# A fused attention and expert kernel on one core: the next attention's loads traced two units sooner, its first copies in program order, small columns made later

## The chip, the cores and the metric

The kernel runs on one core of a Trainium2 chip. The metric is device time in microseconds (us) of one execution. Before the change three runs gave 713.15, 713.35 and 713.98, a median of 713.35. One further execution was recorded by the hardware profiler, and all rows below come from it.

## The reference

Causal attention with a cumulative bias, then two feed-forward layers: a dense one, and four experts whose outputs are added by normalised shares.

```python
# attention: q, k, v (2, 8, 576, 64), s (2, 8, 576)
scores = (q @ k.T) / sqrt(64)
cum    = cumsum(max(s, 0));  bias = -(cum[:, None] - cum[None, :])
scores = where(causal, -1e9, scores + minimum(bias, 0))
attn   = exp(scores - max);  attn /= attn.sum(-1) + 1e-9
x      = (attn @ v)                       # (1152, 512) after joining the heads
# layer 1: w_in (512, 2048), w_out (2048, 512)
h = x @ w_in;  x = where(h > 0, h, exp(min(h, 0)) - 1) @ w_out
# layer 2: 4 experts, w1 (4, 512, 1024), w2 (4, 1024, 512), shares (1152, 4)
p = domain_probs / (domain_probs.sum(-1) + 1e-9)
out = sum over e of p[:, e] * (max(x @ w1[e], 0) @ w2[e])
```

## The kernel before

The 1152 tokens are worked in three groups of 256, 448 and 448. `attention_first` makes the attention of the first group alone. After it `layer1` runs over 16 units of the first layer's weights (a unit is a slice of 128 of the 2048 hidden columns), and then a loop over 32 units (16 to 47) of the expert weights makes layer 2 of the first group. While these 48 units run for the first group, the attention of the second group is made in the background, a few steps per unit. The rest of the program repeats this for the other two groups and is not touched.

**Units.** `slot` traces one unit: the up product (`up1` in layer 1, `up2` in layer 2), then `advance`, which fetches and prepares weights for later units, then the down product of the unit two before (`LAG`). In layer 1 of the first group the weights arrive coded: `fetch_halves` loads 32 halves of 512 KB, `decode_halves` turns each into floats with two ACT and two DVE instructions (L150, L157, L158, L160), and every finished unit is written to HBM (`w_dec`) from POOL's queue for the later groups. Layer 2's units come as plain floats: `fetch` (L97, tile `raw`, 512 KB) is called for unit n + 4 in `advance(n)`, and `prepare` (L103, L87) splits them into a high half on ACT and a low half on DVE (tile `wu`), which the up product needs.

**The background attention.** `attention_parts` returns a list of steps, and `Background` calls them at an even pace between the first and the last unit that `BG_FROM` and `BG_TO` set. The first step, `start`, issues the loads of the eight small pieces (tile `pt`: q, k and v of 128 tokens) and of the first two jobs (tiles `q`, `k`, `cbp`, `v`), 21 DMAs that are all placed behind the last coded half on SP's queue. It also calls `split` for the first item: three copies on ACT (`qs` L478, `kh` L479, `qb` L481) and two subtractions on DVE, which make high and low parts of q and k.

**Order.** The program is traced in the order of the Python code, and a scheduler then may reorder each engine's instructions, with its own picture of how long things take. `tc.keep_in_program_order` forbids this for one instruction; `tc.issue_after` puts a block's instructions behind a given one on its engine. Each engine then works strictly through its list, so an instruction that waits holds up everything after it. SP's list is the DMA queue of all loads; one DMA is issued only when the eighth before it has landed, so there are at most eight under way.

**Small columns.** `cum_columns` makes, with one TensorE transpose and four DVE copies each, columns of the cumulative sums that later items with 64 tokens need. `probabilities_of` loads the experts' shares and normalises them in four small DVE instructions. Before the change both stand in the middle of the first attention.

Of the kernel before, what the change touches and what calls it, by code (L numbers as in the profile page):

```python
# [12 lines left out]
AF = mybir.ActivationFunctionType  # L13
# [21 lines left out]
T2 = GROUPS[1][0]  # L35
NCH = 2 * N2 // 128
# [3 lines left out]

LAG = 2

BG_FROM = [14, 0, 0]
BG_TO = [1, 1, 0]

DEC = [1, 2, 3, 4]
# [7 lines left out]
def tile_kernel(ctx, tc, qT, kT, v, s, w64, w, probs, out):  # L54
# [13 lines left out]
    PE, DVE, ACT, POOL, SP = nc.tensor, nc.vector, nc.scalar, nc.gpsimd, nc.sync  # L68
# [6 lines left out]
    def sb(shape, tag, bufs, dtype=F32):  # L75
        p = (base if tag in BASE else edge if tag in EDGE else l1_pool if tag in L1
             else att_pool[0])
        return p.tile(shape, dtype, tag=tag, name=tag, bufs=bufs)
# [4 lines left out]
    def ps_att():  # L83
        return ps("att", 2)
# [24 lines left out]
    small = [("yh", 1, 1), ("yl", 1, 1)] + [("raw", 3, 1)] * 3 + [("xa", 1, 3), ("ox", 1, 3)]  # L109
# [105 lines left out]
    def cum_columns(b, i):  # L215

        c0, c1 = CHUNKS[b][i], CHUNKS[b][i + 1]
        src, t = sb([B * H, 2, 64], "cum_2", 2), cum_t[b]
        for j in range(2):
            DVE.tensor_copy(src[:, j], cum[:, c0:c1])  # L220
        pt = ps_att()
        PE.transpose(pt[:, :B * H], src.rearrange("p a b -> p (a b)"), ident[:B * H, :B * H])
        DVE.tensor_copy(t, pt[:, :B * H])
        for j in range(2):
            r = slice(64 * j, 64 * j + 64)
            heads = t[r, b * H:(b + 1) * H].rearrange("p (a j) -> p j a", j=2)
            DVE.tensor_copy(cum_p[b][r], heads[:, j])
# [15 lines left out]
    def probabilities_of(t0, n):  # L243

        pr = sb([128, NCH, E], "pr", 2)[:, :n]
        POOL.dma_start(out=pr, in_=probs[t0:t0 + 128 * n].rearrange("(t p) e -> p t e", p=128))
        prs = sb([128, NCH, 1], "prs", 1)[:, :n]
        DVE.tensor_reduce(prs, pr, AX.X, ALU.add)
        DVE.tensor_scalar(prs, prs, 1e-9, None, op0=ALU.add)
        DVE.reciprocal(prs, prs)  # L250
        DVE.tensor_tensor(out=pr, in0=pr, in1=prs.to_broadcast([128, n, E]), op=ALU.mult)
        return pr


    shares = []

    def attention_first(x):


        n = 256  # L260
# [19 lines left out]
        parts, less = (sb([80, n], t, 1, F32R) for t in ("cump", "cumm"))  # L280
# [3 lines left out]
        for t, sign in ((parts, 1.0), (less, -1.0)):  # L284
            POOL.tensor_copy(t[:64], zero)
            high = ACT.activation(t[:B * H], cum[:, 0:n], AF.Copy, scale=sign)
            low = DVE.scalar_tensor_tensor(out=t[64:], in0=cum[:, 0:n], scalar=sign,
                                     in1=t[:B * H].bitcast(F32), op0=ALU.mult, op1=ALU.subtract)
# [9 lines left out]
        def scores(hp):  # L298
            for j in range(2):
                h = 2 * hp + j  # L300
                banks[h] = ps(f"acc{h % 4}", 1) if h < 4 or h > 5 else ps("up", 2)
            for d0, d1 in chunks:
                for j in range(2):
                    r = slice(64 * j, 64 * j + 64)
                    PE.matmul(banks[2 * hp + j][:, d0:d0 + d1], qkv[r, 0, hp, d0:d1],
                              qkv[r, 1, hp, 0:d1], start=d0 == 0, stop=False,
                              skip_group_check=True)
            for j in range(2):
                h = 2 * hp + j
                one = ones[:, h:h + 1]  # L310
                for d0, d1 in chunks:
                    o = banks[h][:, d0:d0 + d1]
                    PE.matmul(o, one.to_broadcast([80, 128]), parts[:, 0:d1],
                              start=False, stop=False, skip_group_check=True)
                    last = PE.matmul(o, less[:, d0:d1], one.to_broadcast([80, d1]),
                                     start=False, stop=d0 > 0, skip_group_check=True)
            return last
# [11 lines left out]
        def normalise(hp):  # L329
            r = sm[:, :, 2 * hp:2 * hp + 2]  # L330
            DVE.tensor_scalar(r, r, 1e-9, None, op0=ALU.add)
            DVE.reciprocal(r, r)
            for h in (2 * hp, 2 * hp + 1):
                for i, (d0, d1) in enumerate(chunks):
                    p = pp[h][:, d0:d0 + d1]
                    scaled = DVE.tensor_scalar(p, p, sm[:, i, h:h + 1], None, op0=ALU.mult)
            return scaled
# [25 lines left out]
            return last  # L363

        with tc.issue_after(keep_warm(12).ins):
            first = scores(0)
            with tc.issue_after(first.ins), tc.issue_after(low.ins):
                cum_columns(0, 4)
                cum_columns(1, 4)
            scores(1)  # L370
            scores(2)
        probabilities(0)
        decode_halves(DEC[0])
        with tc.issue_after(scores(3).ins):
            keep_warm(6)
        probabilities(1)
        with tc.issue_after(normalise(0).ins):
            shares.extend((probabilities_of(0, n // 128), probabilities_of(T2, NCH)))
        with tc.issue_after(transposes(0).ins):
            keep_warm(4)  # L380
        probabilities(2)
# [6 lines left out]
        transposes(2)  # L388
        values(1)
        decode_halves(DEC[2])  # L390
        normalise(3)
        transposes(3)
        values(2)
        values(3)
# [3 lines left out]
    def attention_parts(g, x):  # L398


        items, jobs, small = [], [], []
        for b, chunks, col in JOBS[g]:
            cb = CHUNKS[b]
            q0, q1 = cb[chunks[0]], cb[chunks[-1] + 1]
            for hp in range(HP):
                job = dict(b=b, chunks=chunks, col=col, q0=q0, q1=q1, hp=hp)
# [57 lines left out]
        def split(it):  # L464


            job, j = it["job"], it["j"]
            if j is None or (j, "q") in job:
                return
            q, k = job["q"][:, j], job["k"][:, j]  # L470
            qs = sb([128, q.shape[-1]], "qs", 2, F32R)
            kh = sb([128, k.shape[-1]], "kh", 2, F32R)
            qb = sb([68, q.shape[-1]], "qb", 2, F32R)
            kl = sb([68, k.shape[-1]], "kl", 2, F32R)
            h = job["b"] * H + 2 * job["hp"] + j
            SP.dma_start(out=qb[64:].bitcast(F32), in_=rows_d[h, 2:6, job["q0"]:job["q1"]])
            SP.dma_start(out=kl[64:].bitcast(F32), in_=rows_d[h, 0:4, 0:job["q1"]])
            ACT.activation(qs, q, AF.Copy)  # L478
            ACT.activation(kh, k, AF.Copy)  # L479
            split_lo(qs[64:], q[64:], qs[64:])  # L480
            ACT.activation(qb[:64], q[:64], AF.Copy)  # L481
            split_lo(kl[:64], k[:64], kh[:64])
            job[j, "q"], job[j, "qb"], job[j, "kh"], job[j, "kl"] = qs, qb, kh, kl

# [17 lines left out]
        def normalise():  # L502
            while norm:
                p, sm = norm.pop(0)
                DVE.tensor_scalar(sm, sm, 1e-9, None, op0=ALU.add)
                DVE.reciprocal(sm, sm)
                DVE.tensor_scalar(p, p, sm, None, op0=ALU.mult)

        def scores(it, cut):
            job, i, j = it["job"], it["i"], it["j"]  # L510
            b, hp = job["b"], job["hp"]
            cb = CHUNKS[b]
            d0, d1 = cb[i], cb[i + 1]
            a, e, first, last = cut
            normalise()
            pss = ps_att()
            qk(it, pss, a, e)
            if first:
                it["p"] = sb([128, d1], "p", 4)
                it["low"] = 3.0e38  # L520
                if j is None:
                    it["bias"] = sb([128, d1], "bias", 2)
                    add_bias(it["bias"], job["cump"][:, 0], cum_p[b][:, hp:hp + 1], d0, d1, maskp)
                else:
                    it["bias"] = mask[:, S - d1:]
            p, nm = it["p"], sb([128, 1], "nm", 8)
            DVE.tensor_tensor_reduce(p[:, a:e], pss[:, :e - a], it["bias"][:, a:e], -1.0 / SC,  # L527
                                     it["low"], ALU.add, ALU.min, nm)
            it["low"] = nm
            if last:  # L530
                sm = sb([128, 1], "sm", 4)
                ACT.activation(p, p, AF.Exp, bias=nm, scale=-1.0, accum_out=sm)  # L532
                norm.append((p, sm))
# [46 lines left out]
        def start():  # L580
            with late():
                if small:
                    load_small()
                for job in jobs[:2]:
                    load(job)
            split(items[0])

        parts = [start, lambda: None]
        for n in range(len(items) + 2):
            if n < len(items):  # L590
                it = items[n]
# [158 lines left out]
    class First:  # L750
# [3 lines left out]
        def __call__(self, at):  # L754
            if at > BG_FROM[0]:
                if self.got is None:
# [3 lines left out]
                    xs[1] = sb([128, 2, NCC, N2], "xa", 1, F32R)  # L760
                    self.got = Background(attention_parts(1, xs[1]), BG_FROM[0],
                                          NAB + LAG + E * NCD - BG_TO[0])
# [328 lines left out]
```

## Time and profile before

| What | Value |
|---|---|
| profiled execution, time | 712.33 us |
| its span, first to last instruction | 710.5 us |
| median of three runs | 713.35 us |
| TensorE (PE) busy | 695.7 us, 98% |
| weight loads of TensorE (PEld) busy | 594.1 us, 84% |
| VectorE (DVE) busy | 561.8 us, 79% |
| ScalarE (ACT) busy | 366.9 us, 52% |
| mean granted TensorE clock | 0.997 |
| moved by DMA over the span | 97 MB, mean 137 GB/s |

The shares are means over stages with different limits: in the first 95 us DMA moves three times its mean and ACT and DVE are nearly full, while from 400 us on ACT is a third busy. All that the change touches lies in the first 140 us, so the rows to read are those of that stretch: the timeline of each engine, the list of waits, and windows of a few microseconds. A busy matmul in the record also covers pipelining, so starts of successive blocks tell the pace better than their durations.

### The profile page before, as it was taken

To read this page: it belongs to the slowest core of one execution; us is meant where nothing else is said; L and a number is where in the kernel's file an instruction comes from. 1 tells how busy PE (TensorE), PEld (TensorE's weight loads), DVE (VectorE), ACT (ScalarE), POOL (GpSimd) and SP (SyncE) were. 2 spreads that over 40 slices of the span, in tenths; PEclk is the share of its full clock that TensorE was granted. 3 is DMA by queue.
4 is the path that set the end of the run, shared out by engine and by line. 5 is a ranking of instruction groups with operands and counts; after the bars stand their busy time and mean duration, and the time that the engine had idled before them with its cause. 6 is when DMAs were issued, how large, how long until landed. Compare 5 with 4: busy or idle time off the path is not lost.

```text
span 710.5 us, 10311 instructions
## 1 busy us (share of the span) xinstructions
PE 695.7 (98%) x3670; PEld 594.1 (84%) x3670; DVE 561.8 (79%) x1158; ACT 366.9 (52%) x765; POOL 17.7 (2%) x40
## 2 busy tenths in 40 slices
PE   8999899999999999999999999999999999999997
PEld 7787688887878887887899988888888888888886
DVE  7798679887868988875975469988888888888765
ACT  5897679676667777666754343322222233322320
POOL 5011000000000000000000000000000000000000
PEclk9999999999999999999999999999999999999999
DMA  8999965765674553523552000111111111111002
GB/s 301 410 391 380 318 204 179 226 206 171 185 222 149 173 174 94 161 98 102 226 178 89 1 1 0 60 60 59 60 60 59 60 60 59 60 60 59 1 0 105
DMA packets 40868, 97.00 MB, mean 137 GB/s; under 512 B 4096, under 2 KB 17616, under 8 KB 40816
## 3 DMA queue, kind: packets, MB, share of 16 engines
q1 hardware_dynamic: 38288, 87.67, 37.0%
q0 software_dynamic: 2528, 8.67, 3.0%
q8 instruction: 29, 0.48, 0.3%
q14 instruction: 23, 0.19, 0.1%
HBM read 85.32 MB, written 11.01 MB: 136 GB/s over the span
## 4 chain that ended last, share of the span: by engine, by line
PE 89%; ACT 6%; DVE 2%; DMA 2%; issue 1%; POOL 0%; ACTq 0%; DVEq 0%; POOLq 0%
PE acc L614 39%; PE up L614 17%; PE att L926 11%; PE up L926 8%; PE att L569 3%; PE att L542 3%; ACT z L157 2%; ACT wu L150 2%; DMA raw<-in_w 2%; PE att L497 1%; PE att L490 1%; PE att L492 1%; PE acc L704 1%; PE att L362 1%; PE up L717 1%
## 5 line engine op out<-in xcount | busy, mean ns | idle before, releaser
L614 PE MATMUL acc<-w,h 128*128 128x512 f32 x672 | 172.0, 392 | 0.0
L614 PEld LDWEIGHTS acc<-w,h 128*128 128x128 f32 x672 | 126.1, 188 | 23.0 <-ACT h L936 0.2
L87 DVE TENSOR_TENSOR wu<-raw,wu 128x1024 fp32r<-128x1024 f32 x64 | 78.0, 1220 | 18.7 <-ACT wu L103 18.2
L614 PE MATMUL acc<-gt,wu 128*128 128x448 f32 x384 | 87.8, 372 | 0.0
L671 DVE SCALAR_TENSOR_TENSOR ox<-acc,pr,ox 128x512 f32<-128x512 f32 x105 | 78.5, 748 | 11.4 <-PE acc L614 9.1
L936 ACT ACTIVATE h<-c 128x448 fp32r<-128x448 f32 x48 | 27.4, 573 | 111.2 <-DVE c L942 111.2
L614 PEld LDWEIGHTS acc<-gt,wu 128*128 128x128 f32 x384 | 70.1, 188 | 7.8 <-issue 2.6
L103 ACT ACTIVATE wu<-raw 128x1024 fp32r<-128x1024 f32 x64 | 67.5, 1055 | 16.7 <-PE acc L614 14.5
L926 PE MATMUL att<-S,top 128*128 128x448 f32 x288 | 66.3, 365 | 0.0
L926 PEld LDWEIGHTS att<-S,top 128*128 128x128 f32 x288 | 54.0, 188 | 6.7 <-issue 0.2
L614 PE MATMUL acc<-wu,gt 128*128 128x512 f32 x192 | 56.1, 408 | 0.0
L614 PE MATMUL up<-yh,wu 128*128 128x256 f32 x256 | 53.4, 289 | 0.0
L937 DVE SCALAR_TENSOR_TENSOR h<-c,h 128x448 fp32r<-128x448 f32 x48 | 29.8, 623 | 18.7 <-ACT h L936 18.7
L614 PEld LDWEIGHTS up<-yh,wu 128*128 128x128 f32 x256 | 41.7, 189 | 3.4 <-issue 1.5
L926 PE MATMUL up<-x2a,top 128*128 128x448 f32 x192 | 44.2, 366 | 0.0
L614 PE MATMUL up<-xa,wu 128*128 128x448 f32 x192 | 43.5, 371 | 0.0
L614 PE MATMUL up<-ox,wu 128*128 128x448 f32 x192 | 41.5, 366 | 0.8 <-DVE e L729 0.8
L721 ACT ACTIVATE e<-up 128x448 f32<-128x448 f32 (+1 forms) x48 | 23.5, 489 | 34.0 <-PE up L614 30.2
L532 ACT ACTIVATE p<-p,nm 128x384 f32<-128x384 f32 (+4 forms) x56 | 34.5, 617 | 12.3 <-DVE nm L527 11.9
L926 PEld LDWEIGHTS up<-x2a,top 128*128 128x128 f32 x192 | 35.9, 188 | 4.8 <-ACT p L951 0.6
L936 ACT ACTIVATE h<-up 128x448 fp32r<-128x448 f32 x16 | 8.8, 547 | 59.5 <-PE up L926 59.5
L614 PEld LDWEIGHTS up<-ox,wu 128*128 128x128 f32 x192 | 36.0, 188 | 4.0 <-DVE e L729 1.1
(193 smaller groups left out, 1223.8 us busy)
## 6 DMA issues: line engine op xcount, KB each, us to landing
raw<-in_w SPq DMA_DIRECT2D x38, 512.0 KB
raw<-w_dec SPq DMA_DIRECT2D x32, 512.0 KB
raw<-in_w SPq DMA_DIRECT2D x16, 1024.0 KB
w_dec<-wu POOLq DMA_DIRECT2D x16, 512.0 KB, 7.4
cd<-in_w SPq DMA_DIRECT2D x9, 512.0 KB
k<-in_kT SPq DMA_DIRECT2D x16, 288.0 KB
xa<-in_w SPq DMA_DIRECT2D x5, 512.0 KB
cbp<-cum_d SPq DMA_DIRECT2D x16, 144.0 KB
```

Of the source, the lines that this page charges most:

```text
L87: DVE.tensor_tensor(out=lo, in0=x, in1=hi.bitcast(F32), op=ALU.subtract)
L103: ACT.activation(t[:, 0], x, AF.Copy)
L150: ACT.activation(m, high.bitcast(F32), AF.Abs, scale=2.0 ** -112))
L532: ACT.activation(p, p, AF.Exp, bias=nm, scale=-1.0, accum_out=sm)
L542: PE.transpose(pt[:cb[c + 1] - cb[c], m, :], p[:, cb[c]:cb[c + 1]], ident)
L569: PE.matmul(o[64 * j:64 * j + 64, qs:nq], job["v"][:n, c, 64 * j:64 * j + 64], job["pt"][:n, j, c, qs:nq], start=c == 0, stop=c == n_c - 1)
L614: PE.matmul(o, a[m], b[n], start=first and i == 0, stop=last and i == 2)
L671: DVE.scalar_tensor_tensor(out=o_sb, in0=o, scalar=pr[:, i, e:e + 1], in1=o_sb, op0=ALU.mult, op1=ALU.add)
L721: ACT.activation(e, o, AF.Exp)
L926: PE.matmul(bank, tops[q][:, m, op, cs], x[:, n, c], start=first and c + i == 0, stop=c == 1 and i == 2, skip_group_check=True)
L936: ACT.activation(h[:, 0, u, cs], c, AF.Relu)
L937: DVE.scalar_tensor_tensor(out=h[:, 1, u, cs], in0=c, scalar=0.0, in1=h[:, 0, u, cs].bitcast(F32), op0=ALU.max, op1=ALU.subtract)
```

## The change

`BG_FROM[0]` goes from 14 to 12: the background of the second group's attention begins at unit 12 rather than 14. The first `split` is taken out of `start` and becomes a step of its own, three empty steps after it. The copies of `split` for the small jobs of this group are kept in program order. `cum_columns` and `probabilities_of` move from the first scores and the first normalising to the end of the first attention, behind the last normalising.

```diff
-BG_FROM = [14, 0, 0]
+BG_FROM = [12, 0, 0]
...
-            first = scores(0)
-            with tc.issue_after(first.ins), tc.issue_after(low.ins):
-                cum_columns(0, 4)
-                cum_columns(1, 4)
-            scores(1)
-            scores(2)
+            for hp in range(3):
+                scores(hp)
...
-        with tc.issue_after(normalise(0).ins):
-            shares.extend((probabilities_of(0, n // 128), probabilities_of(T2, NCH)))
+        normalise(0)
...
-        normalise(3)
+        with tc.issue_after(normalise(3).ins):
+            cum_columns(0, 4)
+            cum_columns(1, 4)
+            shares.extend((probabilities_of(0, n // 128), probabilities_of(T2, NCH)))
...
+            place = tc.keep_in_program_order if job in small and g == 1 else lambda i: i
...
-            ACT.activation(qs, q, AF.Copy)
-            ACT.activation(kh, k, AF.Copy)
+            place(ACT.activation(qs, q, AF.Copy))
+            place(ACT.activation(kh, k, AF.Copy))
             split_lo(qs[64:], q[64:], qs[64:])
-            ACT.activation(qb[:64], q[:64], AF.Copy)
+            place(ACT.activation(qb[:64], q[:64], AF.Copy))
...
                 for job in jobs[:2]:
                     load(job)
-            split(items[0])
-
-        parts = [start, lambda: None]
+
+        parts = [start] + [lambda: None] * 3 + [lambda: split(items[0])]
```

SP's queue, from the background's first loads on, before (`pt`, `q`, `k`, `cbp`, `v` are the attention's loads, `raw` are layer 2's weights):

```order
L422 DMA pt<-in_qT 64x8x128 x2
L422 DMA pt<-in_kT 64x8x128
L97 DMA raw<-in_w 128x1024
L422 DMA pt<-in_kT 64x8x128
L97 DMA raw<-in_w 128x1024
L424 DMA pt<-in_v 128x512
L444 DMA q_848<-in_qT 64x2x320 x2
L444 DMA k_851<-in_kT 64x2x576 x2
L452 DMA cbp<-cum_d 64x576 x2
L456 DMA v<-in_v 128x4x128
L462 DMA v<-in_v 64x128
```

The same queue after, from the small pieces' v to the first weights of layer 2:

```order
L422 DMA pt<-in_v 128x512
L442 DMA q_816<-in_qT 64x2x320 x2
L442 DMA k_819<-in_kT 64x2x576 x2
L450 DMA cbp<-cum_d 64x576 x2
L454 DMA v<-in_v 128x4x128
L460 DMA v<-in_v 64x128
L442 DMA q_828<-in_qT 64x2x320 x2
L442 DMA k_831<-in_kT 64x2x576 x2
L450 DMA cbp<-cum_d 64x576 x2
L454 DMA v<-in_v 128x4x128
L460 DMA v<-in_v 64x128
L97 DMA raw<-in_w 128x1024 x3
```

The loads of units 16 and 17 stood among the small pieces' loads; now the loads of units 16, 17 and 18 stand behind all of the attention's loads.

ACT around the first copies, before (`qb`, `qs`, `kh` are the copies of `split`, `e` is layer 1's exponential and what follows it, `wu` and `z` are decoding):

```order
L150 ACTIVATE wu<-raw 128x512
L157 ACTIVATE z_760<-raw 128x512
L481 ACTIVATE qb<-pt 64x128 x2
L478 ACTIVATE qs<-pt 128x128 x2
L721 ACTIVATE e<-up 128x256
L724 ACTIVATE e<-e 128x256
L150 ACTIVATE wu<-xa 128x512
L157 ACTIVATE z_779<-xa 128x512
L150 ACTIVATE wu<-xa 128x512
L157 ACTIVATE z_785<-xa 128x512
L103 ACTIVATE wu<-raw 128x1024
```

ACT around the same place after, up to the exponential of unit 14:

```order
L150 ACTIVATE wu<-raw 128x512
L157 ACTIVATE z_760<-raw 128x512
L720 ACTIVATE e<-up 128x256
L723 ACTIVATE e<-e 128x256
L150 ACTIVATE wu<-xa 128x512
L157 ACTIVATE z_779<-xa 128x512
L150 ACTIVATE wu<-xa 128x512
L157 ACTIVATE z_785<-xa 128x512
L720 ACTIVATE e<-up 128x256
L723 ACTIVATE e<-e 128x256
L720 ACTIVATE e<-up 128x256
L723 ACTIVATE e<-e 128x256
```

Four copies of two items stood ahead of unit 11's exponential; the first copies now come after those of units 11, 12 and 13.

ACT at the end of layer 1, after (`yh` is the high part of layer 1's result, L103 the high half of unit 16's weights):

```order
L723 ACTIVATE e<-e 128x256
L771 ACTIVATE yh<-acc_526 128x256
L771 ACTIVATE yh<-acc_527 128x256
L771 ACTIVATE yh<-acc_528 128x256
L771 ACTIVATE yh<-acc_529 128x256
L103 ACTIVATE wu<-raw 128x1024
L478 ACTIVATE qs<-pt 128x128
L479 ACTIVATE kh<-pt 128x128
L481 ACTIVATE qb<-pt 64x128
```

Before, the splits of units 16 and 17 stood ahead of the exponentials of units 12 and 13; now unit 16's comes behind layer 1's result, and the copies of the next items come behind it.

## Rows read from the trace of the kernel before

**Rows 1.** Waits of PE: line waited for, us in total, times, longest

```profile
PE up L717 <- DVE gt L725: 5.3, 3, 3.9
```

**Rows 2.** Timeline of PE, 66 to 91 us: start, us, engine, line, what

```profile
66.33 1.89 PE L717 MATMUL up<-xf,wu 128*128 128x256 f32 x8
68.05 1.89 PE L704 MATMUL acc<-gt,wu 128*128 128x256 f32 x8
73.88 2.80 PE L717 MATMUL up<-xf,wu 128*128 128x256 f32 x8 [3.94 <-DVE gt L725]
76.47 2.82 PE L704 MATMUL acc<-gt,wu 128*128 128x256 f32 x8
79.77 1.99 PE L717 MATMUL up<-xf,wu 128*128 128x256 f32 x8 [0.48 <-DVE gt L725]
...
83.14 0.41 PE L490 MATMUL att<-kh,qs 128*128 128x128 f32 x1
...
83.50 1.94 PE L717 MATMUL up<-xf,wu 128*128 128x256 f32 x8
...
90.83 0.47 PE L614 MATMUL up<-yh,wu 128*128 128x256 f32 x1
```

**Rows 3.** Timeline of ACT, 70 to 77 us

```profile
70.06 0.51 ACT L481 ACTIVATE qb<-pt 64x128 fp32r<-64x128 f32 x2 [3.63 <-DMA pt<-in_qT]
72.14 0.51 ACT L478 ACTIVATE qs<-pt 128x128 fp32r<-128x128 f32 x2 [1.57 <-DMA pt<-in_qT]
72.56 0.36 ACT L721 ACTIVATE e<-up 128x256 f32<-128x256 f32 x1
...
76.47 1.06 ACT L103 ACTIVATE wu<-raw 128x1024 fp32r<-128x1024 f32 x1 [0.87 <-DMA raw<-in_w]
```

**Rows 4.** Timeline of DVE, 73 to 78 us

```profile
73.40 0.42 DVE L725 SCALAR_TENSOR_TENSOR gt<-up,e 128x256 f32<-128x256 f32 x1 [5.04 <-ACT e L724]
...
77.56 1.23 DVE L87 TENSOR_TENSOR wu<-raw,wu 128x1024 fp32r<-128x1024 f32 x1 [0.71 <-ACT wu L103]
```

**Rows 5.** Windows: length, busy of PE, PEld, DVE, ACT, POOL, PEclk, DMA share, GB/s

```profile
75.00:76.00 1.00, 1.00 (x4) 0.78 (x3) 0.94 (x3) 0.60 (x2) 0.00 (x0) 0.50 1.09 271
...
79.00:80.00 1.00, 0.52 (x3) 0.23 (x2) 0.97 (x4) 0.97 (x3) 0.32 (x1) 1.00 1.04 234
```

**Rows 6.** Timeline of SP's DMA issues, 58 to 93 us

```profile
58.75 1.45 SPq L422 DMA_DIRECT2D pt<-in_qT  x2
...
65.41 0.51 SPq L97 DMA_DIRECT2D raw<-in_w  x1
...
67.82 1.46 SPq L97 DMA_DIRECT2D raw<-in_w  x1
...
88.41 0.99 SPq L97 DMA_DIRECT2D raw<-in_w  x2
...
92.52 0.36 SPq L97 DMA_DIRECT2D raw<-in_w  x1
```

**Rows 7.** Waits of SP's queue, 60 to 100 us

```profile
SPq L452 <- DMA raw<-in_w: 2.4, 1, 2.4
```

**Rows 8.** Windows of the stretch that DMA fills, columns as in rows 5

```profile
10.00:55.00 45.00, 41.70 (x243) 34.48 (x242) 39.87 (x114) 39.42 (x96) 4.84 (x9) 1.00 1.02 395
...
70.00:91.00 21.00, 16.63 (x72) 14.10 (x72) 12.34 (x34) 13.52 (x38) 1.07 (x2) 0.92 1.07 317
91.00:96.00 5.00, 5.00 (x35) 4.61 (x34) 3.02 (x9) 2.85 (x8) 0.00 (x0) 1.00 0.87 310
96.00:100.00 4.00, 4.00 (x28) 3.35 (x26) 3.48 (x12) 2.43 (x8) 0.00 (x0) 1.00 0.04 8
```

**Rows 9.** Window in which the jobs' loads run alone

```profile
86.00:91.00 5.00, 5.00 (x28) 4.43 (x26) 2.75 (x11) 3.38 (x12) 0.00 (x0) 1.00 1.10 260
```

**Rows 10.** Windows of layer 2's first units

```profile
100.00:120.00 20.00, 19.98 (x131) 16.65 (x131) 18.59 (x60) 19.31 (x53) 0.00 (x0) 1.00 0.62 194
120.00:140.00 20.00, 20.00 (x131) 16.16 (x131) 19.01 (x46) 14.50 (x32) 0.00 (x0) 1.00 0.73 220
```

**Rows 11.** Timeline of DVE in the first attention, the columns' copies

```profile
9.59 0.87 DVE L227 COPY cum_p<-cum_t 64x4 f32<-64x4 f32 x4
```

## The prediction

> **What bounds the kernel now.** I read the list of TensorE's waits first. Its one large entry is layer 1's up product waiting for `gt`, 5.3 us in three waits, 3.9 of them at once [rows 1]. The timeline of TensorE gives the place: the down block that starts at 68.05 is followed by nothing until 73.88 [rows 2]. Upwards from there, DVE's `gt` at 73.40 waited 5.04 us for ACT's exponential [rows 4], and ACT's exponential stood at 72.56 behind four copies of the coming attention that had waited 3.63 and 1.57 us for the load of q [rows 3]. So ACT, in order, held up layer 1 for an attention that nobody needed yet. [...]
>
> The second thing to see is that DMA is full all this time: share 1.02 at 10 to 55 us, 1.07 at 70 to 91, and then nothing after 96 [rows 8]. The load of q was issued at 58.75 and let its copies go at 70.06 and 72.14, eleven to twelve microseconds later [rows 3, 6]; the first weights of layer 2 were issued at 65.41 and arrived when ACT could split them, at 76.47 [rows 3, 6], and SP itself waited 2.4 us for them before its next issue [rows 7]. A load here waits for all that stands before it on the queue, so its place on the queue is its arrival.
>
> **The change part by part.**
>
> *The copies leave the exponentials' way.* A block of eight matmuls takes 1.72 us from start to start (66.33 to 68.05, [rows 2]). From 68.05 to unit 16's first product at 90.83 are 22.78 us. In them stand six down and three up blocks, 9 x 1.72 = 15.5 us, and about 1.3 us of attention products (the first pair takes 0.36, 83.14 to 83.50 [rows 2]). The rest, 6.0 us, is the wait, a second one of 0.48 and the slow clock. After the change the first copies follow unit 13's exponential, some 7 us later on TensorE's clock, when q and k have landed. Term: -6.0 us, and layer 1 with one pair of attention products would end at 68.05 + 15.5 + 0.4 = 83.9.
>
> *The loads traced sooner push layer 2's weights back.* They don't leave sooner: before and after, they follow the same last coded half, which waits for decoding. But they now stand ahead of the weights of units 16 and 17, which before had gone out at 65.41 and 67.82 [rows 6]. When do unit 16's weights land? The queue's bytes are the same, so I count from its end. Before, it ran empty at 96, having moved five pieces of layer 2's weights; unit 16's landing after the change leaves four of them still to come, 4 x 0.524 = 2.1 MB. The last 5 us moved 310 x 5 = 1.55 MB, and the 0.55 MB ahead of that went at 260 GB/s, 2.1 us [rows 8, 9]: 91 - 2.1 = 88.9. Reading instead the pace at which SP's loads landed and taking the two weights out gives 89.3. I take 89.2. Bounds: from 70 to 91 were moved 317 x 21 = 6.7 MB, of which 6.1 are needed; at the best long rate, 395 GB/s [rows 8], they take 15.5 us and land at 85.5; at the 260 of the loads alone [rows 9], 23.5 us, 93.5. Then ACT's high half takes 1.06 [rows 3], so TensorE gets unit 16 at about 90.25, against 83.9 when it is ready. Term: +6.35 us (from +2.7 to +10.7). On ACT `yh` is done by then, and the copies of the next items queue behind the waiting split, so there is nothing to fill the wait.
>
> *The start of layer 2.* Before, units 16 and 17 were split 10 us ahead and six attention products were done. Now the third product of unit 16 needs DVE's low half, 1.23 us [rows 4] after the high one, and after it each attention product waits for copies on ACT and subtractions on DVE that stand between unit 16's and unit 17's split. Followed through the new order with durations of the rows, TensorE loses 2 to 3 us more in the next 12 us. Part is made good: from 100 to 140 DVE was 18.6 and 19.0 of 20 us busy [rows 10], so TensorE was not the only limit there, and after the change the attention is further on at that point. Measured on DVE's list the loss is under 1 us. Term: +1.4 (0 to +3).
>
> *The clock.* The gap before was 3.94 us and cost four microseconds at half rate; the new one is 6 us long, so I expect the same fall. TensorE then waits for DVE half of the time anyway. Term: +0.4 (0 to +1.9).
>
> *Columns and shares.* Four copies of 0.87 us [rows 11] and the small instructions of the shares leave the stretch in which DVE limits the first attention, 1.6 us at most; they come back at its end, ahead of the decoding of the second half, up to 1.0 us, and two transposes now take the attention's banks there. POOL's queue, which loads the shares, keeps its order, and so do the small loads of the first split on SP. Either way it is covered by the 6 us that TensorE waits at layer 1's end: 0. Without that cover it would be -1.6 to +1.0.
>
> *Later units.* The background's pace is nearly the same (77 steps over 37 units instead of 74 over 35), and the other reorderings move no wait that I can name: 0, give or take 0.5.
>
> Sum: -6.0 + 6.35 + 1.4 + 0.4 = +2.15 us on the profiled 712.33 (span 710.5 and 1.83 around it), 714.5. The median of the runs stands 1.02 above that execution: 715.5.
>
> [...] The rows give 260 GB/s while the loads of q, k and the sums run alone, each to 64 partitions, and 395 in the long mean of the decoding [rows 8, 9]. [...]
>
> **Rivals.**
>
> *The queue runs faster than I count.* With the loads no longer broken up, and decoding's writes of HBM done earlier, DMA holds 395 GB/s, and unit 16's weights land at 85.5. For it: rows 8 up to 55 us. Against it: 317 and 260 in just these loads. Then -6.0 + 2.7 + 1.0 = -2.3, or 711.0: faster. It decides from a landing before 87.
>
> *The wait and the saving cancel.* Weights at about 88 and a start of layer 2 that is made good by 140 us, since DVE limits there: -6.0 + 5.1 + 0.5 = -0.4, 713.0.
>
> [...]
>
> *The stall only moves.* DVE's `bias`, which reads the first job's `cbp`, stands before unit 14's `gt` and waits for a load that I put at 80.5; `gt` is needed at about 82. If that load came 3 us later, layer 1 would end up to 1.5 us later, but still before the weights: no change of the sum.
>
> **How the numbers follow.** What a measurement of this kernel can tell from no change is 0.2%, 1.4 us. My forecast with its own range of 714.0 to 717.5: 0.52. Cancelling: 0.25, mostly within 0.2%. Faster queue: 0.12. Slower queue: 0.11. That makes faster 0.12, same 0.26, slower 0.62. The range of 8 in 10 takes in most of the cancelling and of the faster queue, 711.6, and ends at 718.8.
>
> **What would show it.** In the profile after: no wait of ACT for q at 66 to 72 and no `gt` wait of 3.9 us (first term); TensorE idle from about 84 to 90 at the first product of `yh`, put down to ACT's split of `raw` or to that load (second term); ACT's first wait for `raw` ending near 89; the clock at 0.50 for some microseconds around 90 to 95; single short waits of TensorE for DVE up to 104. It would be wrong if the wait at layer 1's end is under 3 us, if the weights land before 87, or if layer 2 starts without a ramp.

## The result, and the profile after

The changed kernel takes 721.46 us (median of 4 runs, 719.91 to 723.18) against 713.25 for the kernel before (4 runs, 712.76 to 713.98): a ratio of 1.0116, 95% interval 1.0099 to 1.0133. It is slower, as forecast, but by 8.2 us and not by 2.15, and 721.46 lies above the range of 714.0 to 717.5 and above 718.8. The profiled execution is the slowest of the four (723.18, span 721.4, mean granted clock 0.989).

The waits of TensorE (line waited for, us in total, times, longest) show that the stall of [rows 1] is gone and two others stand in its place:

```profile
PE acc L703 <- DVE gt L724: 3.2, 1, 3.2
PE up L613 <- ACT wu L103: 2.8, 1, 2.8
```

TensorE's timeline, which answers to [rows 2], gives their places. Unit 16's first product of `yh` starts at 94.93; before it was 90.83:

```profile
86.68 5.41 PE L703 MATMUL acc<-gt,wu 128*128 128x256 f32 x16 [3.17 <-DVE gt L724]
94.93 0.58 PE L613 MATMUL up<-yh,wu 128*128 128x256 f32 x1 [2.83 <-ACT wu L103]
```

On ACT (against [rows 3]) nothing waits for q any more; it waits for k, and at layer 1's end for unit 16's weights:

```profile
77.98 0.31 ACT L479 ACTIVATE kh<-pt 128x128 fp32r<-128x128 f32 x1 [2.26 <-DMA pt<-in_kT]
...
93.82 1.06 ACT L103 ACTIVATE wu<-raw 128x1024 fp32r<-128x1024 f32 x1 [1.31 <-DMA raw<-in_w]
```

On DVE (against [rows 4]) a `bias` waits 7.2 us for the sums' rows, and unit 14's `gt` stands right behind it:

```profile
85.81 0.49 DVE L239 TENSOR_SCALAR bias<-cbp,cum_p 128x512 f32<-128x512 f32 x1 [7.20 <-DMA cbp<-cum_d]
86.21 0.42 DVE L724 SCALAR_TENSOR_TENSOR gt<-up,e 128x256 f32<-128x256 f32 x1
```

Four windows of TensorE alone (start and end, length, busy time and matmuls, granted clock, DMA share, GB/s) show what the waits don't: half rate, a granted clock of 0.50, in the first attention at 20 us and for six microseconds at layer 2's start, and a DMA queue that runs partly empty at 50, at a share of 0.37.

```profile
20.00:22.00 2.00, 2.00 (x11) 0.50 1.02 410
...
50.00:52.00 2.00, 2.00 (x11) 1.00 0.37 94
81.00:86.00 5.00, 2.51 (x12) 1.00 1.11 254
...
95.00:101.00 6.00, 5.53 (x23) 0.50 0.35 109
```

The kernel before has clock 1.00 at 20 to 22 us and a share of 0.96 at 50 to 52.

To find where time is lost without a wait, I cut each profiled execution at three starts in TensorE's timeline: unit 16's first product (`up<-yh`), the second group's first product (`up<-xa`), and the third group's (`up<-ox`). All differences are to before. Each row is one execution; the ratios are of the timed runs.

| kernel | unit 16 starts | from there to `xa` | `xa` to `ox` | `ox` to end | ratio (95%) |
|---|---|---|---|---|---|
| before | 90.83 | 125.19 | 120.41 | 374.07 | 1 |
| after | +4.1 | +3.4 | +1.9 | +1.6 | 1.0116 (1.0099–1.0133) |
| cols_only | +2.8 | 0.0 | 0.0 | +0.1 | 1.0043 (1.0030–1.0056) |
| cols_warm | +0.8 | +0.3 | 0.0 | +0.1 | 1.0026 (1.0015–1.0038) |
| cols_back | +0.4 | +4.1 | +1.8 | +0.1 | 1.0095 (1.0080–1.0111) |
| g1_steps | +3.4 | +3.8 | −0.2 | +0.1 | 1.0087 (1.0071–1.0104) |
| after_bias | +4.0 | +3.9 | +1.9 | +0.1 | 1.0116 (1.0099–1.0133) |
| raws_ahead | +2.8 | +0.4 | +1.9 | 0.0 | 1.0085 (1.0071–1.0099) |
| after_job2 | +4.5 | +0.4 | +2.0 | +0.1 | 1.0110 (1.0096–1.0123) |
| after_less | +6.7 | −1.4 | +1.8 | 0.0 | 1.0086 (1.0071–1.0100) |
| copies_in_order | +2.0 | 0.0 | −0.3 | 0.0 | 1.0032 (1.0019–1.0046) |
| splits_late | +3.1 | +5.4 | −0.2 | +0.1 | 1.0118 (1.0092–1.0143) |
| all_late | +0.7 | +6.5 | −0.2 | 0.0 | 1.0064 (1.0045–1.0083) |
| late3 | −1.3 | +5.4 | −0.3 | 0.0 | 1.0045 (1.0032–1.0057) |
| late5 | −5.0 | +7.9 | −0.3 | +0.1 | 1.0026 (1.0017–1.0035) |
| late5j9 | −3.6 | +1.9 | −0.2 | 0.0 | 1.0002 (0.9987–1.0017) |
| late5j13 | −2.8 | +1.6 | −0.2 | +1.5 | 1.0009 (0.9995–1.0023) |
| late3j9 | −4.1 | +6.1 | −0.2 | 0.0 | 1.0018 (1.0004–1.0032) |

The last stretch holds no work that the change touches; two of the 18 executions, the changed kernel's among them, lost 1.5 us in it, so it is variation of an execution and no part of the change. The other three columns make +9.3 for this execution of the changed kernel. The row of late5j9 is its fastest execution (710.39, against a median of 712.13), so it shows that kernel 1.7 us better than its median does.

### The profile page after: what moved, and what is told of

The parts are those of the page before. It is cut to its first block, busy times and chain, and to the rows that moved or that the text cites. A ratio compares the mean times of both kernels' runs of the same rounds, so it can differ in the third digit from the quotient of the medians.

```text
span 721.4 us, 10347 instructions
## 1 busy us (share of the span) xinstructions
PE 704.7 (98%) x3670; PEld 599.1 (83%) x3670; DVE 561.1 (78%) x1158; ACT 366.8 (51%) x765; POOL 17.7 (2%) x40
## 4 chain that ended last, share of the span: by engine, by line
PE 87%; DMA 5%; ACT 4%; DVE 2%; issue 1%; SPq 1%; DVEq 0%; ACTq 0%
PE acc L613 39%; PE up L613 17%; PE att L925 11%; PE up L925 8%; PE att L569 3%; PE att L542 3%; DMA pt<-in_kT 2%; ACT z L157 1%; ACT wu L150 1%; PE att L497 1%; DMA cbp<-cum_d 1%; PE att L490 1%; PE att L492 1%; DMA wu<-in_w 1%; DMA raw<-in_w 1%
## 5 line engine op out<-in xcount | busy, mean ns | idle before, releaser
L613 PE MATMUL acc<-gt,wu 128*128 128x448 f32 x384 | 89.8, 374 | 0.0
L103 ACT ACTIVATE wu<-raw 128x1024 fp32r<-128x1024 f32 x64 | 67.6, 1056 | 30.4 <-PE acc L613 28.7
L613 PEld LDWEIGHTS up<-yh,wu 128*128 128x128 f32 x256 | 43.3, 196 | 5.8 <-ACT wu L103 3.2
L613 PEld LDWEIGHTS acc<-wu,gt 128*128 128x128 f32 x192 | 33.0, 190 | 7.2 <-issue 3.0
```

Of the source, the lines that this page charges most:

```text
L103: ACT.activation(t[:, 0], x, AF.Copy)
L613: PE.matmul(o, a[m], b[n], start=first and i == 0, stop=last and i == 2)
```

## The experiments

**The columns and shares.** Three kernels: the move alone on the kernel before; the changed kernel without it; and the move alone with more filling products (matmuls of `keep_warm`, whose results nobody reads). Here and below the edits are abridged.

```diff
 cols_only = before, with            cols_back = after, without
+            cum_columns(0, 4); cum_columns(1, 4)     (behind normalise(3))
+            shares.extend(...)
 cols_warm = cols_only, with
-            keep_warm(6)
+            keep_warm(11)
```

> The kernel before, with the columns of sums and the shares alone moved to the first attention's end; loads and copies stay as they were. My theory now: the move itself costs the first attention about 3 us (unit 11's up product started at 66.33 before and at 69.31 after the whole change), and since SP's loads follow decoding, q arrives later too and nothing covers it: 716.3 against 713.3 (715.3 to 717.3). Rival, as my prediction had it: the 5 us that TensorE waits in layer 1 cover it: 713.3 (712.5 to 714).

> The changed kernel with the columns and the shares back at their old place: the loads traced sooner and the copies in program order alone. My theory: the 3 us of the first attention go, the waits for the sums' rows and for layer 2's weights stay: 718.5 against 721.5 (717.5 to 719.5). Rival: the landings of the loads set the end of layer 1 whatever the first attention does, and 721 stays. Rival, as my prediction had it: 715.5.

> The kernel before with the columns and shares alone moved (715.0), and 11 instead of 6 filling products on TensorE ahead of the transposes of the first pair of heads, about 1.1 us at full rate, which fall into TensorE's idle 2 us there. My theory: the granted clock no longer falls at 20 to 22 us, where the blocks of the first attention took twice as long, and about 1.5 of the move's 2.8 us come back: 713.5. Rival: what costs is the columns' two transposes on the attention's banks and DVE's instructions at the end, not the clock: 715.

The move alone costs 0.0043 x 712.2 = 3.1 us (715.04), the rest alone 6.8 (718.97); together they make 9.9, where 8.3 are measured. Each of the three ratios is known to about 1 us, so the difference of 1.6 is not resolved, and the profiled executions show no overlap: unit 16 starts 2.8 us later with the move alone, 0.4 with the rest alone and 4.1 with both. cols_back lies within what my theory expected. cols_only costs the 3 us that it expected, though 715.04 is just under its range, since the kernel before ran at 712.2 beside it. cols_warm, at 714.36, lies between its theory and its rival.

The prediction's own term fell as a rival: the cover of 6 us covers nothing. In cols_only TensorE's long wait for `gt` is still 3.7 us (it was 3.9), only later. The reason is what the wait is made of. SP's loads go into buffers that decoding frees (in the changed kernel these loads wait for decoding's last step on DVE six times, 15.7 us in all), and a later first attention makes decoding later. So q, issued at 58.75 before [rows 6], is issued at 61.30 in the changed kernel, and in cols_only at 61.81:

```profile
61.81 1.47 SPq L420 DMA_DIRECT2D pt<-in_qT  x2
```

The stall that was to hide the delay comes from a load that is later by about the same delay.

Where the first attention loses it: TensorE waits 1.96 us for `pt`, the transposed probabilities (1.74 before), and then runs at half rate. The windows of cols_only, then of cols_warm, columns as in the windows above:

```profile
20.00:22.00 2.00, 2.00 (x11) 0.63 1.01 408
22.00:24.00 2.00, 2.00 (x13) 0.51 1.03 422
```

```profile
20.00:22.00 2.00, 2.00 (x20) 1.00 1.01 410
22.00:24.00 2.00, 2.00 (x21) 1.00 1.04 426
```

With five more products in the idle time the clock is 1.00 in the profiled execution, and 1.2 us come back (1.0043 to 1.0026; the intervals overlap). In raws_ahead and after_job2, which have the moved columns without these products, the clock stayed at 1.00 too, so in this place it falls in some executions and not in others; that the products kept it up is likely, not shown. What is left, 0.8 us at unit 16's start or 1.9 by the ratio, was not taken apart. The rows point at the columns' two transposes: in cols_only TensorE's last pair of heads comes behind them and in halves, at 26.66 and 28.47 instead of both from 24.21.

**The queue and the stalls of the changed kernel.** Four edits, each on the changed kernel:

```diff
 raws_ahead: fetch before the attention's loads
+            while g == 1 and fetch_at[0] <= NAB + 1:
+                fetch(fetch_at[0]); fetch_at[0] += 1
             with late(): ...
 after_bias: add_bias on DVE
+    tc.keep_in_program_order(...)   around both instructions
 after_job2: the second job's loads
-                for job in jobs[:2]: load(job)
+                load(jobs[0])           (jobs[1] loaded with split(items[0]))
 after_less: the second job's loads left out
+                for n in ("q", "k", "cump", "v"): jobs[1][n] = jobs[0][n]
```

> The changed kernel with DVE's bias of the sums in program order, so that unit 14's gt no longer stands behind its 7.2 us wait for the sums' rows; ACT's list and the queue stay word for word. My theory: layer 1 then ends some 3 to 5 us sooner, but the weights of unit 16 land where they did, at 93 to 94, and TensorE's wait for them grows by as much: 720.5 against 721.5 (719.5 to 722), so of the two stalls only the later one counts. Rival: DVE's wait is what costs, since the slow clock follows it: 717.5 to 718.5.

> The changed kernel with the weights of units 16 and 17 fetched ahead of the attention's loads again; columns and copies as in the changed kernel. In this order of the program DVE's bias also stands behind the gt of unit 14, not ahead of it. My theory: the wait at layer 2's start and DVE's 7.2 us wait for the sums go, and the saving of 6 us in layer 1 stands, less the 3 us of the moved columns and about 2 us of a later attention: 712.5 (710.5 to 714.5). Rival: the loads of q, k and the sums come later behind the weights and the stall only moves into the first units of layer 2, where DVE is 18 of 20 us busy: 717 to 719.

> The changed kernel with the loads of the second job (q, k, sums, v of one pair of heads, eight DMAs) behind the weights of units 16 and 17 instead of ahead of them; the loads of the small jobs and of the first job stay ahead. My theory: the weights land some 5 us sooner, so TensorE's wait at unit 16 and part of the half-rate stretch behind it go: 717 to 718.5 against 721.5, while DVE's wait for the sums and the 3 us of the moved columns stay. Rival: the queue ends where it did and the rest of the attention is late instead: 721.

> The changed kernel with the second job of the first background reading the first job's q, k, sums and v, so that 1.5 MB of loads are left out of the queue (that pair of heads is then computed from the other's inputs). My theory: the queue's bytes set when layer 2 gets its weights, they land some 5 us sooner (88 to 89 instead of 93.8), and 717 to 718 come out against 721.5; DVE's wait for the sums of the first job is unchanged. Rival: the order of the instructions on ACT, DVE and TensorE costs the time, not the bytes: 720.5 to 722.

after_bias is the clean one: ACT's list and the queue are unchanged, DVE's wait is gone, the ratio is the same to the fourth digit. TensorE's list of waits has one entry where the changed kernel had 3.2 and 2.8:

```profile
PE up L615 <- ACT wu L103: 7.3, 1, 7.3
```

The prediction called itself wrong if that wait were under 3 us; it is 2.8 in the changed kernel only because DVE's stall ahead of it takes the rest. So the stall for `gt` in layer 1 costs nothing of its own: ACT's split of unit 16's weights starts at 93.69, in the changed kernel at 93.82. Moving them ahead (raws_ahead) gives 2.2 us, not the 9 that I expected: the rival held. ACT's split of those weights now stands ahead of unit 12's exponential and waits 6.61 us for them; TensorE waits 5.60 us for `gt`, at 74.8 to 80.4. Moving the second job back (after_job2) lets the weights land at 86.3 and changes no more than 0.4 us (the rival again; the intervals overlap): products of the attention then stand ahead of layer 1's last block and wait 2.8 us for low parts of q, which DVE makes behind the low half of unit 16's weights. Leaving 1.5 MB out (after_less) gives 2.1 us, between theory and rival: ACT splits unit 16's weights at 87.57, but unit 16 starts only at 97.51, behind attention products of which the first waits 3.1 us for DVE. So bytes count, but the order of the lists takes most of the gain back. But for after_less, where the share is 0.95 from 70 to 92, the queue is full until about 90 in all of them (a share of 1.07 or 1.08 at 80 to 90).

**The empty steps in the second background.** The three empty steps and the split as its own step also stand in the background of layer 1 of the second group.

```diff
 g1_steps = after, with
+        if g == 2:
+            parts = [lambda: (start(), split(items[0])), lambda: None]
```

> The changed kernel, with the three empty steps and the split as a step of its own in the first background alone; the second background (during layer 1 of the second group) has its list of steps as before. My theory: of the changed kernel's loss 1.9 us arise between the first product of the second group's layer 1 and that of the third group's (120.4 us before, 122.3 in the three kernels that have the empty steps), so this one gives them back: 719.6 against 721.5. Rival: they come from the tiles' and buffers' places or from where the first background ended, and 721.5 stays.

2.1 us come back (1.0116 to 1.0087), as my theory had it. The intervals overlap by a little, but the table puts it between `xa` and `ox`, where all six kernels with these steps lose 1.8 to 2.0 us and none of the others does. TensorE names no wait of over 0.2 us there in either kernel, is busy throughout, and has the clock at 1.00 and nearly the same number of products (697 and 698). The largest difference is in the attention's products `att<-pt,v` of 256 and 128 columns, 9.4 us busy in the changed kernel and 6.9 in g1_steps and before, with nearly the same mean time of one. That the steps cost the time is shown; how TensorE loses it stays open.

**Where the stall goes.** If ACT's early copies were the cause of the stall, the kernel before should lose it when they alone are put in program order, with nothing else moved.

```diff
 copies_in_order = before, with
+            place = tc.keep_in_program_order if job in small and g == 1 else lambda i: i
+            place(ACT.activation(qs, ...)), likewise kh and qb
 splits_late = that, and in prepare(n) for n < NAB + 3
+        tc.keep_in_program_order(...)   around ACT's split and DVE's
 all_late = that, and the bias in program order
 late3, late5 = that, and for the first background
+            parts = [start] + [lambda: None] * 3 + [lambda: split(items[0])]     (late5: * 5)
```

> The kernel before with one edit: the first attention items' copies on ACT stand in program order, behind the exponentials of units 13 and 14. Loads, weights and columns stay as before. My theory: the stall of 4 to 5 us in layer 1 goes with the slow clock behind it, and up to 2 us come back as a later attention: 708.5 against 713.3 (707 to 711). Rival: layer 2's first 50 us are limited by DVE, which has the attention's work to do whenever layer 1 ends, so the time saved is waited out there: 713 (712 to 714).

> The kernel before, with the attention's first copies and also the splits of the weights of units 16 to 18 (ACT's high half, DVE's low half) in program order, so that on ACT no instruction that waits for one of these late loads stands ahead of an exponential of units 12 to 14. Loads, columns and shares stay as before. My theory now: the stall in layer 1 is a wait of ACT, in order, for whatever late load comes first in its list, and goes only when none is there; unit 16's first product then starts at 86 to 87 against 90.83, and the time is 708.5 to 710 against 712.5. Rival: DVE's bias, which stands ahead of the last gt and waits for the sums, keeps TensorE until about 85 to 86, and with the slow clock behind it unit 16 starts at 90 to 91 again: 712.5.

> As the kernel with copies and splits in program order, and DVE's bias of the sums in program order as well, so that no wait for a late load stands ahead of a gt either. My theory: unit 16 starts at 85 to 87, 4 to 6 us sooner than before, and 707.5 to 709.5 come out against 712.5. Rival: q and k of the attention land at 78 to 80 and its copies stand ahead of unit 15's exponential, and layer 2 is limited by DVE until 140: the saving is 2 us at most, 710.5 to 712.5.

> The kernel before, with copies, splits and bias in program order and three empty steps ahead of the first split of the first background, so that all four last exponentials, unit 15's up product and its gt stand ahead of the first instruction that waits for a late load, on each engine; loads, columns and shares as before. My theory: layer 1's products then run without a stall to about 81, unit 16 starts at 85 to 87 instead of 90.8; in the order that comes of it a chain of attention products stands between units 16 and 17, as in the kernel with copies, splits and bias in program order, where TensorE lost 6 us and its clock after 97 us, so the end is 712 to 716 against 712.5. Rival: with all loads landed the chain does not wait, 707 to 709.

> As the kernel with three empty steps, with five; in its order the attention's products stand one by one between the products of unit 17, as in the kernel before. My theory: unit 16 starts at 85 to 87, the stretch from there to the second group's layer 1 takes 125 to 127 us as before (125.2), and 707 to 710 come out, faster than both kernels. Rival: DVE, 18.6 to 19 of 20 us busy from 100 to 140, has the attention of 35 units to do in 32, and the 4 to 6 us saved are waited out there: 712 to 713.

None of the five is faster than before. late3 came out as expected; in the other four my theory was too hopeful, and they ended above what the rivals allowed too. The rows show the same thing again and again under another name. In copies_in_order ACT waits for unit 16's weights, and TensorE stands longer than before (ACT's timeline, then TensorE's):

```profile
76.27 1.06 ACT L103 ACTIVATE wu<-raw 128x1024 fp32r<-128x1024 f32 x1 [6.41 <-DMA raw<-in_w]
```

```profile
79.58 3.73 PE L718 MATMUL up<-xf,wu 128*128 128x256 f32 x8 [5.73 <-DVE gt L726]
```

In splits_late and all_late no exponential of units 12 to 14 waits; instead an attention product stands ahead of unit 15's up product and waits for k. ACT's and TensorE's rows of all_late:

```profile
80.39 0.31 ACT L483 ACTIVATE kh<-pt 128x128 fp32r<-128x128 f32 x1 [4.44 <-DMA pt<-in_kT]
```

```profile
80.75 0.47 PE L494 MATMUL att<-kh,qs 128*128 128x128 f32 x1 [4.14 <-ACT kh L483]
```

Both lose another 5.4 and 6.5 us behind that: in all_late a chain of small attention products, each waiting 0.3 to 0.5 us for ACT or DVE, stands between units 16 and 17, and the clock is 0.50 at 105 to 110. In late5 layer 1 runs without a stall for `gt`, unit 16 starts 5.0 us sooner, near the 6.0 of the prediction's first term, and then ACT waits for the weights of unit 18, the first behind the attention's loads:

```profile
85.78 0.33 PE L621 MATMUL up<-yh,wu 128*128 128x256 f32 x1
...
95.08 0.39 PE L621 MATMUL up<-yh,wu 128*128 128x256 f32 x1 [2.34 <-ACT wu L104]
```

```profile
93.97 1.06 ACT L104 ACTIVATE wu<-raw 128x1024 fp32r<-128x1024 f32 x1 [3.36 <-DMA raw<-in_w]
```

From unit 16 to `xa` late5 loses 7.9 us. TensorE's waits there make 4.4, the longest being the 2.34 for these weights, and the clock is 0.50 at 98 to 104.

**Fewer bytes ahead of the weights.** The last three kernels keep the order of late5 or late3 and move the second job's loads behind the weights of units 18 and 19 (in late5j13 later still).

```diff
 late5j9 (late5j13, late3j9) = late5 (late5, late3), with
-                for job in jobs[:2]:
+                for job in jobs[:1 if g == 1 else 2]:
+            parts.insert(9, lambda: load(jobs[1]))       (late5j13: 13)
```

> The kernel before with copies, splits and bias in program order and five empty steps, and with the loads of the second job (q, k, sums, v of one pair of heads, 1.5 MB) traced later, so that the weights of units 18 and 19 go out ahead of them. My theory: with five empty steps unit 16 starts at 85.8, 5 us sooner than before, and loses them again because the weights of unit 18 land at 94, behind all loads; with 1.5 MB fewer ahead of them they land near 89, the wait of 2.3 us and the idle time behind it go, and 708 to 710.5 come out against 712.7. Rival: DVE, nearly full from 100 to 140, does not get the attention's work done sooner: 712 to 714.

> The same with the second job's loads traced four steps later, so that they mix with the weights of units 18 to 22. My theory and the rival as in the run with the loads nine steps on: 708 to 710.5, or 712 to 714; should the first job's second pair of heads be late, both versions differ.

> The kernel with three empty steps, with the second job's loads behind the weights of units 18 and 19. It ran at 715.8 without that, with a 2.6 us wait of an attention product for its q. My theory: that wait lies ahead of the moved loads and stays, so 711 to 713. Rival: 715 as before, since the queue ends at the same byte.

late5j9 is 1.7 us faster than late5 (1.0026 to 1.0002; the intervals just touch). In its profiled execution, the fastest of twelve, the stretch behind unit 16 loses 1.9 us instead of 7.9, and TensorE's list has no wait for weights left. Its median of 712.13 is no different from before, and by the ratios 8 us below the changed kernel. Only one of its twelve runs (710.39) met the 708 to 710.5 of my theory; the median gives it to the rival. The other two come out between it and late5, late3j9 at 714.1 nearer to its rival. late3j9 is 1.9 us faster than late3, again with intervals that just touch. So the moved bytes seem to pay, but beyond the kernel before no version got.

## Why the prediction was right in direction and wrong in size

*The copies leave the exponentials' way, −6.0.* Right as a size, but not for the copies by themselves: with them alone in order (copies_in_order) unit 16 starts 2.0 us later. In late5, where the splits and the bias are out of the way too, it starts 5.0 us sooner, with a wait of 1.2 us for DVE left in it. No order gave it as time at the end.

*Weights behind the loads, +6.35.* Right to 1.0 us for the part that it was worked out for: in cols_back the weights landed at 90.15 (89.2 predicted) and unit 16 started at 91.25 (90.25), in ACT's row and TensorE's:

```profile
90.15 1.06 ACT L103 ACTIVATE wu<-raw 128x1024 fp32r<-128x1024 f32 x1 [1.88 <-DMA raw<-in_w]
```

```profile
91.25 0.38 PE L615 MATMUL up<-yh,wu 128*128 128x256 f32 x1 [3.41 <-ACT wu L103]
```

That the start moved by +0.4 and the two terms add up to +0.35 is chance. The forecast start was 0.6 us before the old one, since 0.9 us of attention products (1.3 before, 0.4 after) were to move behind it; the sum counts them. The stall did not stand in one piece, since DVE's `bias` took the first 3.3 us of it. The rival "the stall only moves" named this instruction, put its load at 80.5 instead of 82.9 to 85.8, and said that the sum would not change; after_bias shows that it doesn't.

*The slower queue, 0.11 in the forecast.* The changed kernel's weights landed by 93.82, near the bound of 93.5 that the prediction worked out at 260 GB/s. The nearness is luck for the queue: without the moved columns, in cols_back, the landing is 90.15, so the rest of the delay comes from the first attention. What would slow the queue was the author's estimate, and no run shows it. The forecast looked for a clock of 0.50 around 90 to 95 us; it stood there from 95 to 101.

*The start of layer 2 and the clock, +1.4 and +0.4: mis-sized.* With the 0.9 us of moved products these terms make 2.7 us from unit 16 to `xa`; cols_back loses 4.1 there and the changed kernel 3.4. The step that failed is "TensorE then waits for DVE half of the time anyway". The window from 92 to 100 of cols_back, and of the kernel before:

```profile
92.00:100.00 8.00, 7.49 (x32) 0.57 0.42 136
```

```profile
92.00:100.00 8.00, 8.00 (x54) 1.00 0.43 151
```

TensorE is not waiting half of the time: it is busy 7.5 of 8 us, and gets through 32 matmuls where it did 54. At a clock of 0.57 the eight microseconds are short of 8 x 0.43 = 3.4 us at full rate. This is an estimate from above of what the clock costs, since DVE and ACT, which in the changed kernel are busy for 5.75 and 5.42 of the 6 us from 95 to 101, might have held up a faster TensorE; no run separates the two. In [rows 5] half rate lasted some four microseconds behind one gap. In cols_back the mean of 0.57 is worth 6.9 of the eight microseconds at 0.50, by an estimate, and in the changed kernel the clock is at 0.50 behind each of the two gaps, at 88 to 91 and at 95 to 101. In TensorE's timeline of cols_back a product of 256 columns takes 0.22 us from start to start at 98.18 and 0.12 at 101.05, so full rate is back within nine microseconds of the last wait there, which ended at 92.52.

*Columns and shares, 0: the step that failed most.* 3.1 us alone. "Covered by the 6 us that TensorE waits at layer 1's end" took the landings as fixed in time; they follow decoding, as the prediction's own second term says of the loads. I also had no term for the clock in the first attention, where TensorE already stood idle for 1.74 us, and none for the attention's banks beyond a mention.

*Later units, 0 give or take 0.5.* 2.1 us, from the empty steps in the second background, which the prediction counted only in the first.

With the measured sizes the sum is +0.4 (unit 16's start in cols_back) + 4.1 (from there to `xa`) + 2.1 (second background) + 3.1 (columns) = +9.7. The three columns of the changed kernel's profiled execution make 9.3; the medians say 8.2, 7.1 to 9.5 by the interval. So the parts account for the time to about 1.5 us, which is as far as the intervals go.

*The bounds of the landing, 85.5 and 93.5.* While loads of q, k and the sums ran, the changed kernel's queue moved 254 GB/s at a share of 1.11 (81 to 86 us), which is near the 260 of the later bound and far from the 395 of the earlier one. The landing in cols_back, 90.15, lies between the two.

## What to carry to other kernels

Where an engine's in-order list waits for a load on a full queue, ask what waits next: here removing the waiting instruction mostly let the next one in the list, or on the next engine, wait for a load (ACT 6.41 us in copies_in_order, 4.44 in all_late, 3.36 in late5). So follow the queue to its end, and look for a gain in bytes that can go later rather than in the order of those that wait (here 1.7 and 1.9 us, and only with the order changed first; on the changed kernel a like move gave 0.4 at most). A wait may cover a delay only if its end doesn't depend on the delayed work, so trace the releaser of the cover back to what it is itself issued by. And price each gap of TensorE with the half-rate stretch behind it, from a row of the same kernel (here three to six microseconds at a granted clock of 0.50), for every place where it already stands idle, and every copy of a loop in which the edited code runs.

## What was not expected of the hardware

In the first attention the granted clock stayed at 1.00 behind an idle time of 1.74 us. Behind one of 1.96 or 1.97 us, in the same order of products, the window from 20 to 22 us shows 0.50 in the profiled executions of the changed kernel and g1_steps, 0.63 in cols_only and 0.68 in after_bias, and 1.00 in raws_ahead and after_job2. And half rate at layer 2's start lasted 6.5 us in the changed kernel, 95 to 101.5; by an estimate from the clock that is about 3.3 us of full rate, over half of the 6.0 us of waits that stood before it.
